# Index loads planned longer, first group's scatters behind the gathers, and the last 64 queries of two heads in quarters of TensorE

## The chip, the core and the metric

The kernel runs on one core of a Trainium2 chip. The metric is the device time of one execution in microseconds (us); the lower the better. Times of single instructions and waits are from the profile of one execution.

## The reference

The kernel computes three layers in one launch.

```python
# 1. attention, 4 batches x 8 heads, 576 queries and keys, 64 dims
scores = scale * q @ k.T
keep   = scores >= max(scores) - tau
attn   = softmax(where(keep, scores, -1e9));  x = attn @ v
# 2. dense layer on 2304 rows: 512 -> 2048 -> 512
h = x @ w_in;  x = (h * sigmoid(h)) @ w_out
# 3. one of 8 experts per row: 512 -> 1024 -> 512
e = argmax(normalised(x) @ normalised(expert_emb).T / tau2)
out[row] = gate(row) * (relu(x[row] @ w1[e]) @ w2[e])
```

## The kernel before

**Attention.** Heads go in pairs: 16 pairs (4 batches, 4 pairs each), 64 dims of one head on partitions 0 to 63 and of the other on 64 to 127. The 576 queries of a head are four chunks of 128 and a rest of 64. `score_pe` (L496) makes the scores of one chunk. For chunks 0 to 3 the two heads' products stand in the upper and lower 64 rows of TensorE and alternate, each head into its own bank of PSUM. The rest of both heads is one chunk, number 4: 64 queries of the first head and 64 of the second as the 128 columns of the stationary operand. In q, as the host lays it out, each of them has zeros in the other head's 64 rows, so one product over all 128 rows gives both. In the first eight pairs (`WIDE`, 72 steps) the 576 keys go in four pieces of 144, later in two of 288. Then DVE takes the maximum of each row (L519), ACT the exponential (L525), DVE masks and sums (L540), TensorE transposes (L577, L585, L593, L597) and multiplies with v (L669).

**Dense layer.** `moe_block` (L681) does six of sixteen hidden groups of 128 for a block of 256 rows beside the attention of later batches; `tail` (L1183) does the rest: three early blocks, then the other ten hidden groups of all nine blocks. Each hidden group is a product (L1117), tanh on ACT (L1337), a gate on DVE (L1342), a split into a high half on ACT (L1351) and a low half on POOL or DVE (L1354), and the second product (L1369).

**Experts.** The eight experts are sorted by the number of their rows. A table in DRAM collects the row numbers of each expert: POOL scatters 128 rows at a time into it (L1593). `turned` (L1842) then loads the indices of a group of rows (L1853, on SP), gathers the rows by them (L1860, indirect DMA from POOL), transposes them on TensorE (L1869) and splits them (L1875 on ACT, L1880 on DVE). `compute` (L1898) does the expert's two products (L1117 and L1928 or L1932), scales (L1967 on DVE, L1963 on ACT) and scatters the rows into the output (L1955, POOL). There are nine groups, 0 to 8. The weights of an expert are loaded in eight parts by SP (L1827) and split by ACT (L1094) and by DVE or POOL (L1098).

**What sets the order.** Every step is a task of a planner (`Plan`, L105) with an engine, a planned time, what it comes after, the buffers it takes and gives, and a rank. `Plan.run` (L220) walks through a planned time line: at each point it takes the task that can start first, among those that can start at about the same time the one of the lowest rank, and issues it then. So the planned times decide the order in which the instructions stand on each engine; on the chip each engine goes through its list in that order and waits where something is missing. `more` is a planned time from the end of a task to where its result is there (the way of a DMA). Tasks with `alt` go to the second engine if it is free earlier.

```python
t = plan.task("sp", 0.45, indices, [...], rank=..., more=1.8)      # L1882: index load
score = plan.task("pe", 1.18, partial(self.score_pe, ...), ...)    # L904
plan.task("pool", 1.03, partial(scatter, t, o), (x,), ...)         # L2001: into the output
```

Of the kernel before, what the change touches and what calls it, by code (L numbers as in the profile page):

```python
# [55 lines left out]
NBLK = NTOK // BLK  # L56
# [8 lines left out]
HALF = [slice(0, 64), slice(64, 128)]  # L65
# [195 lines left out]
class Kernel:  # L261
# [234 lines left out]
    def score_pe(self, st, ch, ws, uses):  # L496

        nc = self.nc
        for h, (w, use) in enumerate(zip(ws, uses)):
            w.nm = f"{ch}{h}" + st.nm  # L500
            bank = 3 if use.tag[0] == "B" else 0
            if use.wide:
                at = 512 * bank + 4 * APART * use.slot
                w.S = self.flat[:, at:at + 4 * APART].rearrange("p (a x) -> p a x", x=APART)[:, :, :PIECE]
            else:
                w.S = self.banks[:, bank:bank + 2, :288]
        lhsT = st.o.q[:, 128 * ch:128 * ch + 128]
        n, c = w.S.shape[1:]
        for a in range(n):
            for h, w in enumerate(ws):  # L510

                rows = HALF[h] if ch < 4 else slice(None)
                nc.tensor.matmul(  # L513
                    w.S[:, a], lhsT=lhsT[rows], rhs=st.o.k[rows, c * a:c * a + c], start=True, stop=True
                )

    def score_max(self, w):
# [367 lines left out]
    def attend(self, plan, pair, n, o, x_there):  # L885

        steps = self.steps(pair, o)
        st = steps[0][0]
# [4 lines left out]
        for a, step in enumerate(steps):  # L893
            s = 9.0 * n + a
            _, ch, h = step
            if h == 0:

                pe = []
                for i in range(2 if ch < 4 else 1):
                    w = Obj()  # L900
                    w.use = Token(f"{'AB'[i]}{(9 * n // 2 + n % 2 + (a + 1) // 2) % 2 if s < WIDE else 0}")
                    w.use.wide = s < WIDE
                    pe.append(w)
                score = plan.task(  # L904
                    "pe", 1.18, partial(self.score_pe, st, ch, pe, [w.use for w in pe]),
                    o.there + self.last_s + ([] if s < WIDE else self.last_wide),
                    tuple(w.use for w in pe), (o.k_use, o.q_use), rank=s - 0.6, slack=0.1, mode="scores",
                )
                self.last_s = [score]
                for x in (int(s) - 1, int(s)):  # L910
                    if x in self.held:
                        plan.link(score, self.held.pop(x))
            w = pe[h]
            scores, t = w.use, score
# [4 lines left out]
            t = plan.task("act", 0.84, partial(self.score_exp, w), (mx,), (use[2],), rank=s - 2, slack=0)  # L919
# [8 lines left out]
            for i, (tag, turn, pieces) in enumerate(self.turns(step)):  # L928
# [3 lines left out]
                give = [self.more_banks["T"]] if tag == "T" else []  # L932
# [871 lines left out]
    def experts(self, plan, const, last_job, u0, parts, halves, x2_taken, x_taken, seen, places, before):  # L1804
        nc = self.nc
# [36 lines left out]
        def turned(i, x_before):  # L1842

            rank, base, nt, p = SUBS[i]
            w = subs[i]
            n = nt * p
            r = units[i] - 4.0
            w.x_use = Token("X")
            w.x_there = []

            def indices():
                w.idx = self.pool.tile([128, nt, 2], I32, tag=f"idx{i}", bufs=1, name=f"idx{i}")
                nc.sync.dma_start(  # L1853
                    out=w.idx[:p],
                    in_=tbl[bass.ds(regs[rank], 1), base:base + nt * p].rearrange("o (p t) c -> (o p) t c", t=nt),
                )

            def gather(t, o):
                o.xg = self.pool.tile([128, ROW], F32, tag="s", bufs=BUFS["s"], name=f"xg{i}_{t}")[:, :DM]
                nc.gpsimd.indirect_dma_start(  # L1860
                    out=o.xg[:p], out_offset=None, in_=self.x2[:, :],
                    in_offset=bass.IndirectOffsetOnAxis(ap=w.idx[:p, t, 0:1], axis=0),
                )

            def turn(t, o, bank):
                if t == 0:
                    w.x = self.x_tiles(w.x_use, f"xe{i}", n)
                for kk in range(4):
                    nc.tensor.transpose(  # L1869
                        self.banks[:, bank.slot, p * kk:p * kk + p], o.xg[:p, 128 * kk:128 * kk + 128], self.ident[:p, :p]  # L1870
                    )

            def hi(t, bank):
                src = self.banks[:, bank.slot, :4 * p].rearrange("p (k x) -> p k x", k=4)
                nc.scalar.activation(out=w.x[0][:, :, p * t:p * t + p], in_=src, func=AF.Copy)  # L1875

            def lo(t, bank):
                to = (slice(None), slice(None), slice(p * t, p * t + p))
                src = self.banks[:, bank.slot, :4 * p].rearrange("p (k x) -> p k x", k=4)
                nc.vector.tensor_tensor(out=w.x[1][to], in0=src, in1=w.x[0][to].bitcast(F32), op=ALU.subtract)  # L1880

            t = plan.task("sp", 0.45, indices, [reg_there[rank]] + sum(places if i else places[:NBLK - 2], []), rank=r - (12 if i < 2 else 5), more=1.8)  # L1882
            us = p / 240 + 0.06, p / 240 + 0.08
            for j in range(nt):
                o, s_use, bank = Obj(), Token("s"), Token("M")
                x = plan.task("pool", 1.03, partial(gather, j, o), [t] + gathers[-1:], (s_use,), rank=r - (12 if i < 2 else 2) + 0.1 * j)
                gathers.append(x)
                x = plan.task("dma", 0.0, Obj, (x,), more=2.9)
                turns.append(plan.task(
                    "pe", 4 * p / 1200 + 0.01, partial(turn, j, o, bank), [x] + turns[-1:] + (x_before if j == 0 else []),  # L1890
                    (bank, w.x_use) if j == 0 else (bank,), (s_use,), rank=r,
                ))
                if j == 0:
                    x_taken.append(turns[-1])
                x = plan.task("act", us[0], partial(hi, j, bank), turns[-1:], (), (bank,), rank=r)
                w.x_there.append(plan.task("dve", us[1], partial(lo, j, bank), (x,), (), (bank,), rank=r))

        def compute(i):  # L1898
            rank, base, nt, p = SUBS[i]
            w = subs[i]  # L1900
# [89 lines left out]
            for t in range(nt):  # L1990
                o, row_use = Obj(), Token("rows")
                if by_rows:
                    bank, x = y_use[t], end[t]
                else:
                    bank = Token("M")
                    x = plan.task("pe", 0.43, partial(turn, t, bank), end, (bank,), (yT_use,), rank=r)
                x = plan.task(
                    "dve", 0.62, partial(scale, t, o, bank), [x] + before, (row_use,), (bank,), rank=r, alt=("act", 0.6)
                )
                before = [x]  # L2000
                plan.task("pool", 1.03, partial(scatter, t, o), (x,), give=(row_use,), rank=r, more=2.9)  # L2001

        before = weights(0, before)
        turned(0, x_taken[-1:])
# [78 lines left out]
```

## Time and profile before

| | us |
|---|---|
| median of three runs | 1062.93 |
| the three runs | 1062.93, 1062.95, 1058.68 |
| the profiled execution's own time | 1058.08 |
| its span from the first to the last instruction | 1056.3 |
| PE busy | 970.1 |
| DVE busy | 696.2 |
| ACT busy | 538.6 |
| POOL busy | 415.7 |

The span is one execution of the program on the chip. PE is TensorE's matmul, PEld its weight load, SP issues the DMAs of the loads and POOL the indirect ones. A wait is the idle time of an engine just before an instruction, with the instruction that ended it. A fp32 product shows as two MATMUL rows. TensorE's clock is granted at one of two levels, 1.2 and 2.4 GHz, which the profile gives as 0.50 and 1.00.

### The profile page before, as it was taken

The page shows a single profiled execution, that of the slowest core. Times are in us where ns is not written, and L with a number is a line of the kernel's source. Part 1 is how long each engine was busy: PE and PEld are TensorE (multiplying, and loading weights), DVE is VectorE, ACT ScalarE, POOL GpSimd, SP SyncE. Part 2 cuts the span into 40 slices and gives each one's busy share as a digit, 9 for nine tenths or more (in the row PEclk, how much of TensorE's full clock was granted, in tenths as well). Part 3 has the DMA queues.
Part 4 walks back from the last instruction along what each step waited for, and adds up shares of the span by engine and source line. Part 5 has one row for each costly group of instructions (what it writes and reads, how often), then busy time and mean ns, then how long its engine had stood idle before and what let it go on. Part 6 is the DMA issues. An engine that isn't in the chain of part 4 may idle for free. (4 is left out here: it accounts for less than half of the span.)

```text
span 1056.3 us, 18778 instructions
## 1 busy us (share of the span) xinstructions
PE 970.1 (92%) x6667; PEld 817.1 (77%) x6667; DVE 696.2 (66%) x1654; ACT 538.6 (51%) x1252; POOL 415.7 (39%) x406
## 2 busy tenths in 40 slices
PE   4878879999999899989999999999896999999995
PEld 4555566667667676878899889999786999899994
DVE  5779877878787886463388878777637445645521
ACT  4777776767676665363533333433534444344510
POOL 3565521445556640120154554443415434243210
PEclk9899999999999999999999999999998999999998
DMA  3234212454545421450532120212617745455400
GB/s 129 99 129 144 94 46 82 143 170 138 162 151 175 152 97 50 151 180 30 181 118 81 42 81 31 66 57 79 185 49 226 216 145 172 142 162 174 140 32 16
DMA packets 77633, 124.55 MB, mean 118 GB/s; under 512 B 11748, under 2 KB 38676, under 8 KB 77537
## 3 DMA queue, kind: packets, MB, share of 16 engines
q1 hardware_dynamic: 73089, 112.93, 33.8%
q0 software_dynamic: 4448, 10.40, 3.2%
q8 instruction: 53, 0.87, 0.3%
q14 instruction: 43, 0.35, 0.1%
HBM read 96.66 MB, written 27.45 MB: 117 GB/s over the span
## 5 line engine op out<-in xcount | busy, mean ns | idle before, releaser
L519 DVE TENSOR_REDUCE m<-banks 128x1 f32<-128x576 f32 x144 | 105.0, 752 | 34.0 <-PE banks L513 28.1
L540 DVE SCALAR_TENSOR_TENSOR P<-banks,m,e 128x576 f32<-128x576 f32 x128 | 103.5, 815 | 29.0 <-ACT e L525 16.2
L1094 ACT ACTIVATE whe<-rawe 128x512 fp32r<-128x512 f32 x128 | 76.6, 625 | 88.7 <-PE banks L1932 29.2
L1098 DVE TENSOR_TENSOR wle<-rawe,whe 128x512 fp32r<-128x512 f32 x93 | 68.4, 760 | 79.6 <-ACT whe L1094 72.7
L525 ACT ACTIVATE e<-banks,m 128x576 f32<-128x576 f32 x144 | 105.5, 733 | 14.0 <-PE banks L513 9.7
L513 PE MATMUL banks<-k,q 64*128 64x144 f32 (+3 forms) x792 | 98.2, 353 | 12.2 <-DVE m L519 4.9
L295 ACT ACTIVATE p<-banks 128x512 f32<-128x512 f32 (+2 forms) x164 | 75.3, 475 | 58.2 <-PE banks L577 39.3
L577 PE MATMUL banks<-ident,P 128*128 128x128 f32 x512 | 83.9, 288 | 22.3 <-ACT p L295 13.6
L1337 ACT ACTIVATE t<-banks 128x256 f32<-128x256 f32 x108 | 41.2, 382 | 122.7 <-PE banks L1117 119.5
L1117 PE MATMUL banks<-xs_6h,wh 128*128 128x256 f32 x360 | 102.4, 284 | 0.0
L1117 PE MATMUL banks<-xs_6h,wl 128*128 128x256 f32 x360 | 102.0, 283 | 0.0
L1117 PE MATMUL banks<-xs_6l,wh 128*128 128x256 f32 x360 | 101.9, 283 | 0.0
L577 PEld LDWEIGHTS banks<-ident,P 128*128 128x128 f32 x512 | 57.3, 144 | 52.4 <-ACT p L295 20.9
L669 PE MATMUL banks<-p,v 128*64 128x256 f32 (+3 forms) x640 | 91.6, 421 | 0.0
L513 PEld LDWEIGHTS banks<-k,q 64*128 64x128 f32 (+1 forms) x792 | 69.2, 195 | 28.1 <-DVE m L519 6.8
L1342 DVE SCALAR_TENSOR_TENSOR g<-t,banks 128x256 f32<-128x256 f32 x108 | 45.2, 419 | 58.8 <-ACT t L1337 47.4
L1098 POOL TENSOR_TENSOR wle<-rawe,whe 128x512 fp32r<-128x512 f32 x35 | 45.7, 1310 | 95.1 <-ACT whe L1094 79.2
L669 PEld LDWEIGHTS banks<-p,v 128*64 128x64 f32 (+1 forms) x640 | 41.4, 137 | 41.6 <-issue 19.5
L1117 PEld LDWEIGHTS banks<-xs_6h,wh 128*128 128x128 f32 x360 | 68.8, 191 | 3.1
L1117 PEld LDWEIGHTS banks<-xs_6l,wh 128*128 128x128 f32 x360 | 68.6, 190 | 3.0
L348 POOL TENSOR_TENSOR wa<-wa,wr 128x512 int32<-128x512 int32 x32 | 41.2, 1286 | 73.0 <-DVE wa L343 41.2
L1117 PEld LDWEIGHTS banks<-xs_6h,wl 128*128 128x128 f32 x360 | 68.5, 190 | 0.0
(560 smaller groups left out, 2833.1 us busy)
## 6 DMA issues: line engine op xcount, KB each, us to landing
rawe<-moe_w SPq DMA_DIRECT2D x64, 512.0 KB
wraw<-moe_w_in SPq DMA_DIRECT2D x16, 512.0 KB
wraw<-moe_w_out SPq DMA_DIRECT2D x16, 512.0 KB
wd<-wa SPq DMA_DIRECT2D x20, 256.0 KB
raw<-wd SPq DMA_DIRECT2D x10, 512.0 KB
q<-q SPq DMA_DIRECT2D x15, 320.0 KB
v<-v SPq DMA_DIRECT2D x16, 288.0 KB
x_dram<-t SPq DMA_DIRECT2D x16, 288.0 KB
```

Source lines behind the costliest of these rows:

```text
L295: self.nc.scalar.activation(out=out, in_=src, func=AF.Copy)
L348: nc.gpsimd.tensor_tensor(out=o.a, in0=o.a, in1=o.r, op=ALU.add)
L513: nc.tensor.matmul(w.S[:, a], lhsT=lhsT[rows], rhs=st.o.k[rows, c * a:c * a + c], start=True, stop=True)
L519: self.nc.vector.tensor_reduce(out=w.m[:, 0:1], in_=w.S, axis=AX.XY, op=ALU.max, negate=True)
L525: self.nc.scalar.activation(out=w.e, in_=w.S, func=AF.Exp, bias=w.m[:, 0:1])
L540: self.nc.vector.scalar_tensor_tensor(out=P.rearrange("p (a x) -> p a x", a=w.S.shape[1]), in0=w.S, scalar=w.m[:, 1:2], in1=w.e, op0=ALU.i ...
L577: nc.tensor.transpose(T[:, 128 * j:128 * j + 128], st.P[ch][:, c:c + 128], self.ident)
L669: nc.tensor.matmul(w.av[HALF[h], :nq], lhsT=st.o.vn[rows, k, :], rhs=st.pts[part][rows, k, :], start=(j == 0), stop=(j == 4),)
L1094: self.nc.scalar.activation(out=o.tiles[0][:, 2 * a:2 * a + 2], in_=o.raw[:, 2 * a:2 * a + 2], func=AF.Copy)
L1098: self.on[on].tensor_tensor(out=o.tiles[1][:, to], in0=o.raw[:, to], in1=o.tiles[0][:, to].bitcast(F32), op=ALU.subtract)
L1117: self.nc.tensor.matmul(h[:, :n], lhsT=lhs(a, kk), rhs=z[:, kk, :], start=(kk == 0 and i == 0), stop=(kk == 3 and i == 2))
L1342: nc.vector.scalar_tensor_tensor(out=o.g, in0=o.t, scalar=1.0, in1=self.banks[:, use.slot, :BLK], op0=ALU.add, op1=ALU.mult)
```

## The change

Chunk 4 becomes two products a piece: 64 rows by 64 columns in the upper left quarter of TensorE, and 64 by 64 in the lower right one, both into the same bank as before, on partitions 0 to 63 and 64 to 127. Its planned time goes from 1.18 to 0.65. The planned way of an index load goes from 1.8 to 3.5. The output scatters of group 0 come after the last gather that is planned before them, which is that of group 1. Six lines come in above L513, so that below it a line of the changed kernel has a number higher by six.

```diff
@@ score_pe
         lhsT = st.o.q[:, 128 * ch:128 * ch + 128]
         n, c = w.S.shape[1:]
+        if ch == 4:
+
+            for a in range(n):
+                for x in HALF:
+                    nc.tensor.matmul(
+                        w.S[x, a], lhsT=lhsT[x, x], rhs=st.o.k[x, c * a:c * a + c], start=True, stop=True
+                    )
+            return
         for a in range(n):
             for h, w in enumerate(ws):
-
-                rows = HALF[h] if ch < 4 else slice(None)
                 nc.tensor.matmul(
-                    w.S[:, a], lhsT=lhsT[rows], rhs=st.o.k[rows, c * a:c * a + c], start=True, stop=True
+                    w.S[:, a], lhsT=lhsT[HALF[h]], rhs=st.o.k[HALF[h], c * a:c * a + c], start=True, stop=True
                 )
@@ attend
                 score = plan.task(
-                    "pe", 1.18, partial(self.score_pe, st, ch, pe, [w.use for w in pe]),
+                    "pe", 1.18 if ch < 4 else 0.65, partial(self.score_pe, st, ch, pe, [w.use for w in pe]),
@@ turned
-            t = plan.task("sp", 0.45, indices, [reg_there[rank]] + sum(places if i else places[:NBLK - 2], []), rank=r - (12 if i < 2 else 5), more=1.8)
+            t = plan.task("sp", 0.45, indices, [reg_there[rank]] + sum(places if i else places[:NBLK - 2], []), rank=r - (12 if i < 2 else 5), more=3.5)
@@ compute
-                plan.task("pool", 1.03, partial(scatter, t, o), (x,), give=(row_use,), rank=r, more=2.9)
+                plan.task(
+                    "pool", 1.03, partial(scatter, t, o), [x] + (gathers[-1:] if i == 0 else []), give=(row_use,), rank=r, more=2.9
+                )
```

The planned times move instructions on all engines from the first pair to the second expert group; behind that (from expert group 3 on) the lists are the same. Three places are shown, each as the list of one engine before and now. Names end in a number of the buffer.

ACT, where the dense layer's early blocks begin after the last attention pair. `xs0_6h` is the high half of a block's input that a DMA brings, `wh` a high half of weights, `po5` the result of block 5, `t17_0` the tanh of the first hidden group of block 7, `ga7_0h` the high half that the second product waits for. Before:

```order
L1264 ACTIVATE xs0_6h_4658<-xc00_4660 128x2x256
L1094 ACTIVATE wh06_4691<-raw06_4664 128x512 x2
L1094 ACTIVATE wh16_4702<-raw16_4667 128x512
L1264 ACTIVATE xs0_6h_4658<-xc02_4680 128x2x256
L1094 ACTIVATE wh16_4702<-raw16_4667 128x512
L750 ACTIVATE po5_0_4723<-banks_99 128x512
L750 ACTIVATE po5_1_4729<-banks_99 128x512
L1337 ACTIVATE t17_0_4740<-banks_99 128x256
L1094 ACTIVATE wh08_4745<-raw08_4672 128x512 x2
L1337 ACTIVATE t17_1_4762<-banks_99 128x256
L1351 ACTIVATE ga7_0h_4768<-g17_0_4748 128x256
```

Now:

```order
L1270 ACTIVATE xs0_6h_4712<-xc00_4714 128x2x256
L1100 ACTIVATE wh06_4747<-raw06_4718 128x512
L756 ACTIVATE po5_0_4752<-banks_99 128x512
L756 ACTIVATE po5_1_4761<-banks_99 128x512
L1270 ACTIVATE xs0_6h_4712<-xc02_4736 128x2x256
L1343 ACTIVATE t17_0_4778<-banks_99 128x256
L1100 ACTIVATE wh06_4747<-raw06_4718 128x512
L1100 ACTIVATE wh16_4791<-raw16_4722 128x512
L1343 ACTIVATE t17_1_4798<-banks_99 128x256
L1357 ACTIVATE ga7_0h_4804<-g17_0_4786 128x256
```

The two results of block 5 and the weight halves no longer stand between the second input half (`xc02`) and the first tanh; between the tanh and `ga7_0h` there are still two weight halves and a tanh.

POOL, at the end of the last dense block (8), where the first expert group's rows are gathered. `gs8_8l` and `gs8_9l` are the low halves of hidden groups 8 and 9, `xg0_0` the first gather of group 0, which waits for the index load `idx0`. Before:

```order
L1593 DMA table_76<-ids_5705,at6_8163 19456x16 x2
L1354 TENSOR_TENSOR gs8_7l_8341<-g18_7_8307,gs8_7h_8340 128x256
L1354 TENSOR_TENSOR gs8_8l_8392<-g18_8_8379,gs8_8h_8391 128x256
L1860 DMA xg0_0_8413<-x2_75,idx0_8355 128x512
L1354 TENSOR_TENSOR gs8_9l_8421<-g18_9_8405,gs8_9h_8420 128x256
L1860 DMA xg0_1_8444<-x2_75,idx0_8355 128x512
```

Now:

```order
L1360 TENSOR_TENSOR gs8_7l_8291<-g18_7_8287,gs8_7h_8290 128x256
L1104 TENSOR_TENSOR wle0_0_8425<-rawe0_0_8314,whe0_0_8424 128x512 x2
L1360 TENSOR_TENSOR gs8_8l_8464<-g18_8_8447,gs8_8h_8463 128x256
L1866 DMA xg0_0_8507<-x2_75,idx0_8404 128x512
L1360 TENSOR_TENSOR gs8_9l_8502<-g18_9_8483,gs8_9h_8501 128x256
L1599 DMA table_76<-ids_5737,at7_8466 19456x16 x2
L1866 DMA xg0_1_8567<-x2_75,idx0_8404 128x512
```

The low half `gs8_9l` stands behind the gather as before, and two weight halves have come in ahead of it. On PE, of the 24 products of hidden groups 10 and 11 (`wh010`, `wl010`) three stood ahead of the products with group 8, three between those and the products with group 9, and 18 behind; now all 24 stand ahead of group 8's, and three of the next between the two. So PE has 21 more products to do before it needs `gs8_9l`. On SP one more register load stands ahead of the load of `idx0`.

POOL, at the end of expert group 0. `xg1_0` to `xg1_2` are the three gathers of group 1, `yr0_0` and `yr0_1` the scaled rows of group 0. Before:

```order
L1860 DMA xg1_0_8966<-x2_75,idx1_8931 96x512
L1860 DMA xg1_1_8980<-x2_75,idx1_8931 96x512
L1955 DMA out<-yr0_0_8978,idx0_8355 2304x512
L1860 DMA xg1_2_8987<-x2_75,idx1_8931 96x512
L1955 DMA out<-yr0_1_8982,idx0_8355 2304x512
L1098 TENSOR_TENSOR wle1_1_8704<-rawe1_1_8651,whe1_1_8703 128x512
L1098 TENSOR_TENSOR wle1_2_8719<-rawe1_2_8669,whe1_2_8718 128x512
```

Now:

```order
L1866 DMA xg1_0_9028<-x2_75,idx1_8979 96x512
L1866 DMA xg1_1_9030<-x2_75,idx1_8979 96x512
L1866 DMA xg1_2_9032<-x2_75,idx1_8979 96x512
L1104 TENSOR_TENSOR wle1_0_8727<-rawe1_0_8686,whe1_0_8726 128x512
L1961 DMA out<-yr0_0_9024,idx0_8404 2304x512
L1961 DMA out<-yr0_1_9026,idx0_8404 2304x512
```

The third gather no longer stands behind a scatter, and of two weight halves on POOL one is left. DVE, which had a weight half ahead of each of the three low halves of group 1's rows (`xe1l`, L1880) and two more ahead of them all, now has four ahead of the first and one between the first and the second.

## Rows read from the trace of the kernel before

**Rows 1.** Page, part 1: busy time, share of the span and instructions.
```profile
PE 970.1 (92%) x6667; PEld 817.1 (77%) x6667; DVE 696.2 (66%) x1654; ACT 538.6 (51%) x1252; POOL 415.7 (39%) x406
```

**Rows 2.** Busy time by stretch: length; engines with counts; granted clock, DMA share, GB/s.
```profile
20.00:190.00 170.00, 136.92 (x1165) 97.69 (x1165) 134.73 (x267) 121.00 (x279) 75.83 (x60) 0.95 0.30 97
...
746.10:749.50 3.40, 3.40 (x11) 2.94 (x12) 0.00 (x0) 0.00 (x0) 2.76 (x3) 0.50 0.90 303
...
797.30:807.60 10.30, 7.41 (x30) 6.82 (x31) 5.99 (x6) 3.52 (x7) 6.83 (x7) 0.50 0.93 279
...
452.60:456.00 3.40, 3.40 (x14) 3.01 (x13) 3.25 (x8) 3.27 (x9) 2.13 (x3) 0.50 0.95 297
```

**Rows 3.** Timeline, 447 to 452: start, length, engine, instruction, [idle before <-releaser].
```profile
447.28 0.63 ACT L1264 ACTIVATE xs_6h<-xc 128x512 fp32r<-128x512 f32 x1 [1.29 <-DMA xc<-x_dram]
447.82 0.61 ACT L1094 ACTIVATE wh<-raw 128x512 fp32r<-128x512 f32 x1
...
449.29 0.38 ACT L1337 ACTIVATE t<-banks 128x256 f32<-128x256 f32 x1
...
450.86 0.43 ACT L1351 ACTIVATE ga_0h<-g 128x256 fp32r<-128x256 f32 x1
...
451.35 0.49 PE L1369 MATMUL banks<-who,ga_0h 128*128 128x512 f32 x1 [3.02 <-ACT ga_0h L1351]
```

**Rows 4.** Timeline of PE, 311 to 314: a long wait inside the attention stage.
```profile
312.59 0.66 PE L577 MATMUL banks<-ident,P 128*128 128x128 f32 x4 [1.77 <-DVE P L540]
```

**Rows 5.** Timeline of POOL, 728 to 752: the first gather of group 0.
```profile
743.96 1.26 POOL L1860 DMA_INDIRECT xg<-x,idx  x1 [4.29 <-DMA idx<-table]
```

**Rows 6.** Timeline of PE, 726 to 752: 33 products in a row, then the wait.
```profile
734.85 0.36 PE L1117 MATMUL banks<-xs_6h,wh 128*128 128x256 f32 x1
...
738.88 0.39 PE L1369 MATMUL banks<-wh,gs_7h 128*128 128x512 f32 x1
...
746.03 0.74 PE L1369 MATMUL banks<-wh,gs_9l 128*128 128x512 f32 x1 [3.37 <-POOL gs_9l L1354]
```

**Rows 7.** Source L1799, SP's register loads: duration min/median/max in ns, first and last start.
```profile
L1799 SPq TENSOR_LOAD <-eint x8: 262/270/485, 733.8 to 740.8; - x8
```

**Rows 8.** Timeline of POOL, 780 to 815: gathers of group 1, scatters of group 0.
```profile
790.54 0.93 POOL L1860 DMA_INDIRECT xg<-x,idx  x1 [0.31 <-issue]
793.38 1.01 POOL L1955 DMA_INDIRECT out<-yr,idx  x1 [1.92 <-DVE yr L1967]
794.69 1.10 POOL L1860 DMA_INDIRECT xg<-x,idx  x1 [0.30 <-issue]
```

**Rows 9.** Timeline of PE, 792 to 802: the transposes of group 1.
```profile
793.75 0.55 PE L1869 MATMUL banks<-ident,xg 96*128 96x96 f32 x4 [0.42 <-DMA xg<-x,idx]
799.61 0.90 PE L1869 MATMUL banks<-ident,xg 96*128 96x96 f32 x4 [5.30 <-DMA xg<-x,idx]
801.09 0.61 PE L1117 MATMUL banks<-xe1h,whe 128*128 128x288 f32 x1 [0.58 <-ACT xe1h L1875]
```

**Rows 10.** Timeline of DVE, 792 to 802: scaled rows, weight halves, low halves.
```profile
792.35 1.44 DVE L1967 TENSOR_SCALAR yr<-banks,idx 128x512 f32<-128x512 f32 x2 [1.19 <-issue]
793.71 1.28 DVE L1098 TENSOR_TENSOR wle<-rawe,whe 128x512 fp32r<-128x512 f32 x2
...
796.44 3.74 DVE L1098 TENSOR_TENSOR wle<-rawe,whe 128x512 fp32r<-128x512 f32 x1
```

**Rows 11.** Timeline of PE, 185 to 187: chunk 4 before, and what follows it.
```profile
185.02 1.25 PE L513 MATMUL banks<-k,q 128*128 128x144 f32 x8
186.10 0.60 PE L577 MATMUL banks<-ident,P 128*128 128x128 f32 x4
```

**Rows 12.** Timeline of PE, 190 to 193: a chunk of two heads in 64 rows each.
```profile
191.08 1.24 PE L513 MATMUL banks<-k,q 64*128 64x288 f32 x8
192.25 0.49 PE L669 MATMUL banks<-p,v 128*64 128x320 f32 x2
```

**Rows 13.** PE by form, 30 to 440: count, busy us, mean ns of one, idle before.
```profile
L669 PE MATMUL banks<-p,v 64*64 64x320 f32 x64 | 12.1, 455 | 0.0
```

## Prediction

> **What bounds the kernel now.** I read the page's busy times first: TensorE is busy for 970.1 us of the span, 92%, DVE for 66% [rows 1]. So time is to be had only where TensorE idles or runs at half clock, and an edit that touches none of these can only cost. Next the busy times by stretch [rows 2]: from 20 to 190 us, the stage of the wide attention groups, TensorE is busy 136.92 of 170 us; there its 33 us of idle time belong to a chain over all engines (DVE alone 134.73), not to one wait. Later it hardly idles, except in three long waits. Each has its row with the engine that ended it: 3.02 us at 451.35 for ACT's high half of a gate [rows 3], 3.37 us at 746.03 for POOL's low half of a gate [rows 6], and 5.30 us plus 0.58 at 799.61 for a gather [rows 9]. And each is followed by a stretch at a granted clock of 0.50: 452.6 to 456.0, 746.1 to 749.5, 797.3 to 807.6, in which TensorE was busy 3.40, 3.40 and 7.41 us [rows 2]. At 1.00 the first two would have taken half as much, 1.7 us each. A wait of 1.77 us elsewhere had no stretch of half clock that I found behind it [rows 4]. So a wait costs its own length and perhaps as much again through the clock, and the change moves work in front of all three.
>
> **The change part by part.** The order lists show that it does move instructions, so "nothing changes" is not open.
>
> *The wait at 451.* Before, ACT took the second input half at 447.28, then weight halves and the two results of block 5, and only at 449.29 the tanh; the high half that TensorE waits for came at 450.86, 1.57 us after the tanh [rows 3]. Now the tanh stands right behind the input half, so it can start where a weight half started, 447.82. Between it and the high half stand as before two weight halves and a tanh, so 1.57 us again: 449.4 instead of 450.86. That takes 1.5 off the wait, which is then some 1.5 us, under the 1.77 that left the clock alone. Late instead are the weight halves for the next hidden groups, by one or two times 0.61, and TensorE has products of block 7 in front of those. The clock: none of the 1.7 us or all of it; I take half, -0.9, as DMA waits and weight halves keep the place thin. Together **-2.4** (bounds -1.5 and -3.2).
>
> *The wait at 746.* The chain is: index load, first gather (which waited 4.29 us for it [rows 5]), then the low half behind the gather on POOL, then TensorE. The longer planned way of the index load does not shorten that; it makes the planner put work in front of it. TensorE now has 21 more products to do before it needs the low half. 33 products in a row took 738.88 - 734.85 = 4.03 us, 0.122 each [rows 6]: 2.6 us. Against it one more register load stands ahead of the index load on SP. One takes 0.27 us, and eight of them started between 733.8 and 740.8, so 1.0 apart with what they wait for [rows 7]; I take 0.6. The wait falls by 2.6 - 0.6 = 1.9, to 1.45. Those 21 products were behind the wait before, so nothing is late for them; POOL's table scatter, which now stands between two gathers, and the two weight halves ahead of it lie under the same index wait. At 1.45, less than 1.77 [rows 4], I expect the clock to stay up: -1.7. Together **-3.6** (bounds -1.5, where the clock falls all the same, and -3.7).
>
> *The wait at 799.* Before, the second gather issued at 790.54, then a scatter that waited 1.92 for DVE and stood at 793.38, and only at 794.69 the third gather [rows 8]. Now the third follows the second: 790.54 + 0.93 + 0.30 = 791.8. From issue to the transpose that waited for it took 3.2 us for one gather (790.54 to 793.75) and 4.9 for another (794.69 to 799.61) [rows 8, 9]. So the rows would be there at 795.0 to 796.7, 2.9 to 4.6 earlier. But the change also puts four weight halves of 0.64 us (1.28 for two [rows 10]) on DVE ahead of the first low half of these rows, and one behind it. The scaled rows end at 793.7 [rows 10], so the first low half can start at 796.4, the third not before 798.3. One weight half here was stretched to 3.74 us [rows 10], beside POOL's work; with part of that the third comes at 799.6. The products, which started at 801.09 [rows 9], then start 1.5 to 2.8 earlier; I take -2.1. The two scatters of group 0 are some 2 us later, and nobody reads the output; their buffers are needed again in group 1, over 10 us on. In 797.3 to 807.6 TensorE was busy 7.41 us at half clock [rows 2], worth up to 3.7 less what was waited anyway; since a wait of some 3 us stays I take -1.0. Together **-3.1** (bounds -1.5, and -2.8 - 3.7 = -6.5).
>
> *The quarters.* A chunk 4 took 186.10 - 185.02 = 1.08 us to the start of the next operation: eight rows (four pieces, two rows each) some 0.13 apart [rows 11]. A chunk of two heads with 64 rows each, of as many columns in all, took 192.25 - 191.08 = 1.17 [rows 12]. The products with v already run in quarters: 64 rows, mean 455 ns, make 29.1 us if laid end to end, and 12.1 us busy [rows 13], so the two quarters run side by side, each at the length of its columns. Two quarters do in one pass what the one product with zeros did in one pass: no column is saved. I price a group at 1.17, +0.09, and with 16 groups **+1.4** (bounds 0 and, if quarters take turns, +1.08 each).
>
> The Trainium skill, page TensorEngine Tiling (Array Packing), section Theoretical Speedup, gives dimensions of at most 64 up to twice the speed. By that a group would take 0.54 and the sum would be 8.6 lower; that is rival B below. The trace so far does not bear it out for two quarters against one full product, since the product with zeros already holds both heads.
>
> *The planned 0.65.* The planner now thinks that chunk 4 ends 1.17 - 0.65 = 0.52 us sooner than it does. So what it issues behind it (the maximum on DVE, the next work on TensorE) is laid out too early, and an in-order engine waits behind it. Only the eight wide groups have idle time that this disturbs. The bounds are 0, where the idle time of 33 us takes it up, and 16 x 0.52 = 8.3. Next to them I have no row; the idle share of 19% [rows 2] lets me take 0.2 for each of eight groups, **+1.6**.
>
> **The sum:** -2.4 - 3.6 - 3.1 + 1.4 + 1.6 = -6.1. From the profiled execution's 1058.08 that is 1052.0. That execution lies with the fastest of the three runs; the median is 4.9 us above it, and from there the sum is 1056.8. As I can't say which of these levels the changed kernel will show, I predict the middle, **1054.4**, 0.8% under the median. A difference of 0.5%, 5.3 us, is about what a measurement can tell from none.
>
> **The rivals.**
>
> A. *The waits are only exchanged.* At 799 DVE's weight halves take the place of the gather, at 746 the index load comes a whole microsecond later, and the clock falls in all three places as before. For it: every stretch here has a DMA share of 0.90 to 0.95 [rows 2], and DVE's stretched half of 3.74 [rows 10]. Against it: 21 products are real work moved into the gap. The places then give -1.5 - 1.5 - 1.5, the quarters and plan take +3.0: -1.5, so 1056.6 to 1061.4. Chance 0.20, same.
>
> B. *Quarters run in half the time*, as the plan says (0.65). Then the +3.0 falls away, and 16 groups give 0.54 each, 8.6: 1058.1 - 9.1 - 8.6 = 1040, or 1045 if the wide stage, which waits for others, keeps its half. Against it: the two quarters of [rows 13] each take their full length. Chance 0.08, faster.
>
> C. *Quarters take turns*, because both write into one bank at once. Each group then doubles, +1.08, 16 times +17.3: 1058.1 - 9.1 + 1.6 + 17.3 = 1067.9. Slower. For it: the full chunks send each head into its own bank. Against it: both heads' products with v write one bank, and their rows overlap [rows 13]. It decides as soon as a group takes over 1.6 us. Chance 0.05. The Trainium skill, same page, section Restrictions and Gotchas, says that different row tiles write to different banks; by it this rival would hold, and the overlap in the trace speaks against it.
>
> D. *The wide stage loses*: slower. The planner's error of 0.52 us passes down the chain for all 16 groups, 8.3, the quarters cost 1.4, and the tail gives 1.5 at each of three places, -4.5, with no clock: +5.2, so 1063.3 from the profiled execution, 1068.1 from the median. The place is 20 to 190 us, and the point is where its 33 us of idle time grow by more than the tail gains. For it: everything there is issued in an order made from planned times, and DVE is 79% busy [rows 2]. Against it: an error of half a microsecond is small beside 33 us of slack. Chance 0.10.
>
> **How the numbers follow.** The forecast has 0.57: 0.40 of it faster, 0.17 within 0.5%, where a clock dip stays or the level is that of the median. With B faster is 0.48; with A same is 0.37; C and D make slower 0.15. The range: at the low end all three places at their best, -3.2 - 3.7 - 6.5 = -13.4, with costs between +1.4 and +3.0, give 1046.1 to 1047.7; 1047. At the high end 1064 takes in A from the median and D from the profiled execution. B, C and D from the median stay outside, under 0.2.
>
> **What would show it.** Right: a wait near 1.5 us at about 450 and at about 745, with a clock of 1.00 behind the second; the third gather of group 1 issued right behind the second; chunk 4 in 16 rows at about 1.17 us; idle time of TensorE from 20 to 190 within 2 us of 33. Wrong: a granted clock of 0.50 behind all three places (A), a chunk 4 at 0.6 (B) or above 1.6 (C), or over 5 us more idle time in the wide stage (D).

## The result and the profile after

The changed kernel takes 1068.05 us in the median of 20 runs (1062.67 to 1072.05), the kernel before 1060.88 in 20 runs of the same series. The ratio is 1.0068, with a 95% interval of 1.0051 to 1.0085: about 7 us **slower**, where 6 us faster was forecast. The time lies above the range. One of the 20 runs of the kernel before took 5201.01 us and has no part in the ratio.

The two profiled executions took 1058.08 and 1070.64 us, 12.6 apart, where the medians are 7.2 apart. So what follows, read from these two traces, shows where the time went, but makes the loss look some 5 us larger than it is.

The page's busy times of the changed kernel, in the columns of [rows 1]:

```profile
PE 986.4 (92%) x6763; PEld 820.8 (77%) x6763; DVE 700.8 (66%) x1639; ACT 540.0 (51%) x1260; POOL 422.6 (40%) x413
```

TensorE has 96 rows more (the quarters) and is busy 16.3 us longer. The span grew by 12.6, so over the whole kernel idle time is not what grew. The busy times by stretch say where. The attention stage is taken from the start of the span to the last product with v, which stood at 428.5 us and now stands at 444.6; the columns are those of [rows 2]. Before:

```profile
0.00:186.00 186.00, 142.83 (x1201) 102.89 (x1202) 140.38 (x279) 125.92 (x286) 79.91 (x68) 0.95 0.32 103
0.00:428.50 428.50, 375.51 (x2830) 270.80 (x2832) 332.44 (x667) 287.54 (x670) 195.16 (x165) 0.98 0.38 122
```

After, in the same two stretches (the first ends with the last scores of a wide group) and in the one from 20 to 190:

```profile
0.00:200.40 200.40, 153.35 (x1239) 109.03 (x1241) 140.51 (x282) 127.09 (x290) 75.53 (x64) 0.86 0.28 91
0.00:444.60 444.60, 392.68 (x2928) 275.50 (x2928) 329.23 (x656) 289.58 (x678) 196.48 (x168) 0.93 0.36 118
...
20.00:190.00 170.00, 135.25 (x1107) 94.26 (x1108) 126.18 (x253) 113.21 (x263) 70.22 (x55) 0.88 0.27 87
```

The attention stage is 16.1 us longer. Its idle time of TensorE is 428.5 - 375.5 = 53.0 before and 444.6 - 392.7 = 51.9 now. Its busy time is 17.2 us more for the same products (at most 1.6 of it is the quarters' own time, worked out below), at a mean granted clock of 0.93 instead of 0.98. So over the stage the loss is paid in clock. Most of it, 200.4 - 186.0 = 14.4 us, lies ahead of 200 us, where the clock went from 0.95 to 0.86. Up to there idle time grew too, from 186.0 - 142.8 = 43.2 to 200.4 - 153.4 = 47.0 us; behind that TensorE waits some 5 us less than before, so the sum over the stage stays.

Behind the attention stage the kernel took 1056.3 - 428.5 = 627.8 before and takes 1068.9 - 444.6 = 624.3 now, 3.5 us less. That is less than half of the 9.1 that the three waits were to bring, and no more than single executions differ: the run of the quarters alone (below), which has the old order there, took 1056.2 - 432.9 = 623.3. The three places in the changed kernel, TensorE's timeline:

```profile
465.90 0.50 PE L1375 MATMUL banks<-who,ga_0h 128*128 128x512 f32 x1 [1.52 <-ACT ga_0h L1357]
...
763.38 0.50 PE L1375 MATMUL banks<-wh,gs_9l 128*128 128x512 f32 x1 [0.57 <-POOL gs_9l L1360]
...
807.00 1.19 PE L1875 MATMUL banks<-ident,xg 96*128 96x96 f32 x8 [0.73 <-DMA xg<-x,idx]
...
808.77 0.40 PE L1123 MATMUL banks<-xe1h,whe 128*128 128x288 f32 x1 [0.58 <-ACT xe1h L1881]
...
811.98 0.61 PE L1123 MATMUL banks<-xe1l,whe 128*128 128x288 f32 x1 [2.81 <-DVE xe1l L1886]
...
821.13 0.61 PE L1938 MATMUL banks<-he_0h,whe 128*128 128x288 f32 x1 [4.11 <-ACT he_0h L1921]
...
822.58 0.61 PE L1938 MATMUL banks<-he_0l,whe 128*128 128x288 f32 x1 [0.84 <-DVE he_0l L1924]
```

and the stretches behind them (length, TensorE busy, ..., granted clock):

```profile
467.70:471.10 3.40, 3.40 (x15) 3.10 (x14) 3.15 (x8) 2.32 (x7) 1.27 (x1) 0.50 0.62 210
755.00:775.00 20.00, 18.63 (x129) 16.68 (x128) 14.26 (x31) 12.95 (x31) 13.49 (x12) 1.00 0.73 233
809.00:815.80 6.80, 3.99 (x17) 3.82 (x17) 4.22 (x8) 1.54 (x3) 4.66 (x5) 0.50 0.95 306
819.30:826.10 6.80, 4.13 (x15) 3.81 (x16) 4.59 (x7) 4.44 (x9) 1.27 (x1) 0.50 0.79 224
```

The wait near 451 is 1.52 instead of 3.02 [rows 3], but a half-clock stretch still follows. The one of 3.37 near 746 [rows 6] is down to 0.57, and there the clock stays at 1.00. The 5.30 for the third gather [rows 9] became 0.73 and 2.81; then a wait of 4.11 came up that was 0.24 in the kernel before, in the lines behind those of [rows 9]:

```profile
808.26 0.40 PE L1932 MATMUL banks<-he_0h,whe 128*128 128x288 f32 x1 [0.24 <-ACT he_0h L1915]
809.71 0.40 PE L1932 MATMUL banks<-he_0l,whe 128*128 128x288 f32 x1 [1.05 <-DVE he_0l L1918]
```

ACT's timeline names what ended the 4.11:

```profile
819.63 1.15 ACT L1100 ACTIVATE whe<-rawe 128x512 fp32r<-128x512 f32 x2 [3.06 <-DMA rawe<-moe_w]
820.68 0.39 ACT L1921 ACTIVATE he_0h<-banks 128x288 fp32r<-128x288 f32 x1
```

The high half `he_0h` stands on ACT behind two weight halves, and those waited 3.06 us for a load. The waits shown from the transposes to `he_0l` make 0.73 + 0.58 + 2.81 + 4.11 + 0.84 = 9.1 us, where before they were 5.30 + 0.58 + 0.24 + 1.05 = 7.2; the third place brought nothing.

### The profile page after: what moved, and what is told of

The parts are those of the page before. It is cut to its first block, busy times and chain, and to the rows that moved or that the text cites. A ratio compares the mean times of both kernels' runs of the same rounds, so it can differ in the third digit from the quotient of the medians.

```text
span 1068.9 us, 18974 instructions
## 1 busy us (share of the span) xinstructions
PE 986.4 (92%) x6763; PEld 820.8 (77%) x6763; DVE 700.8 (66%) x1639; ACT 540.0 (51%) x1260; POOL 422.6 (40%) x413
## 5 line engine op out<-in xcount | busy, mean ns | idle before, releaser
L1104 DVE TENSOR_TENSOR wle<-rawe,whe 128x512 fp32r<-128x512 f32 x93 | 64.2, 716 | 80.1 <-ACT whe L1100 71.0
L295 ACT ACTIVATE p<-banks 128x512 f32<-128x512 f32 (+2 forms) x172 | 80.8, 488 | 69.1 <-PE banks L583 52.3
L583 PE MATMUL banks<-ident,P 128*128 128x128 f32 x512 | 86.7, 294 | 22.7 <-DVE P L546 11.3
L675 PE MATMUL banks<-p,v 128*64 128x256 f32 (+3 forms) x640 | 99.2, 450 | 0.0
L519 PE MATMUL banks<-k,q 64*128 64x144 f32 (+1 forms) x704 | 81.5, 360 | 5.7 <-DVE m L525 3.1
L675 PEld LDWEIGHTS banks<-p,v 128*64 128x64 f32 (+1 forms) x640 | 44.2, 148 | 47.8 <-issue 26.7
L519 PEld LDWEIGHTS banks<-k,q 64*128 64x128 f32 x704 | 56.7, 199 | 20.7 <-issue 7.9
```

The lines of the kernel that those rows point to most:

```text
L295: self.nc.scalar.activation(out=out, in_=src, func=AF.Copy)
L519: nc.tensor.matmul(w.S[:, a], lhsT=lhsT[HALF[h]], rhs=st.o.k[HALF[h], c * a:c * a + c], start=True, stop=True)
L583: nc.tensor.transpose(T[:, 128 * j:128 * j + 128], st.P[ch][:, c:c + 128], self.ident)
L675: nc.tensor.matmul(w.av[HALF[h], :nq], lhsT=st.o.vn[rows, k, :], rhs=st.pts[part][rows, k, :], start=(j == 0), stop=(j == 4),)
L1104: self.on[on].tensor_tensor(out=o.tiles[1][:, to], in0=o.raw[:, to], in1=o.tiles[0][:, to].bitcast(F32), op=ALU.subtract)
```

## The experiments

Two theories at first. **P**: the planned 0.65 gives the wide stage another order, and that order costs the clock. **Q**: the quarters do, because they keep less of TensorE at work, or cost time themselves. Each run was timed in rounds beside the kernel before on the same chip; a ratio is against that.

### Only the planned time, only the quarters, only the tail, and all but the planned time

```diff
# e1_plan_only: the old product
-                    "pe", 1.18, partial(self.score_pe, ...
+                    "pe", 1.18 if ch < 4 else 0.65, partial(self.score_pe, ...
# e2_quarters_only: the quarters in score_pe, "pe", 1.18
# e3_tail_only: old product at 1.18; more=3.5; scatters of group 0 behind gathers[-1:]
# e4_true_plan: the changed kernel with
-                    "pe", 1.18 if ch < 4 else 0.65, partial(self.score_pe, ...
+                    "pe", 1.18, partial(self.score_pe, ...
```

Expected of the first: 

> Chunk 4 keeps the one product with zeros over 128 rows; only its planned time is 0.65 instead of 1.18. Theory P (the planned time reorders the wide stage, and the order brings the stretches of half clock): 12 to 16 us slower than the kernel before, ratio 1.011 to 1.015, with 45 us or more of granted clock 0.50 before 200 us (17 us in the kernel before). Theory Q (quarter products, which keep a smaller part of TensorE at work, bring the half clock): no slower than 1.002, about 17 us of half clock before 200 us.

Of the second: 

> Chunk 4 in quarters, planned at 1.18 as before: the order of every engine is that of the kernel before, only the products differ. Theory P: +1.5 us from the quarters' own time (1.13 against 1.08 in eight groups, 1.12 against 0.97 in eight), ratio 1.000 to 1.003, half clock before 200 us as in the kernel before. Theory Q: 12 us or more slower, ratio above 1.010.

Of the third: 

> Old product, planned at 1.18; only the index load's planned way of 3.5 and the scatters of group 0 behind the gather. If the tail's gain stands by itself (theory P and Q alike): 3 to 5 us faster, ratio 0.995 to 0.997, with the wait near 746 below 1.8 us and the one near 800 below 4. If the gain at the gather needed the other order of the attention stage too: ratio 0.999 to 1.001.

Of the fourth: 

> The changed kernel with chunk 4 planned at 1.18, so with quarters, the index latency and the scatter order, but the old order of the attention stage. Theory P: the sum of the two runs before, 1.5 to 3.5 us faster than the kernel before, ratio 0.996 to 0.999, so some 9 us faster than the changed kernel. Theory Q: as slow as the changed kernel, ratio 1.006 to 1.012.

| | median us | ratio | 95% interval |
|---|---|---|---|
| planned 0.65 alone | 1068.97 | 1.0081 | 1.0055 to 1.0108 |
| quarters alone | 1058.49 | 0.9994 | 0.9966 to 1.0022 |
| index load and scatters alone | 1054.35 | 0.9937 | 0.9916 to 0.9958 |
| all but the planned 0.65 | 1053.83 | 0.9943 | 0.9920 to 0.9966 |
| the change | 1068.05 | 1.0068 | 1.0051 to 1.0085 |

P holds and Q falls. A number in the planner, with every product as it was, makes the kernel slower by as much as the whole change; the quarters cost nothing that these runs can tell; and the change without that number is faster than the kernel before by 0.57%. The loss came out smaller than the 1.1% that P expected, the tail's gain larger than expected. The stretches of the attention stage, of 0.65 alone, the quarters alone and the tail alone, each to its last product with v:

```profile
0.00:442.30 442.30, 388.70 (x2830) 278.71 (x2832) 329.75 (x656) 290.55 (x678) 196.84 (x168) 0.93 0.37 118
```
```profile
0.00:432.90 432.90, 381.92 (x2927) 268.34 (x2928) 330.08 (x667) 287.00 (x670) 195.38 (x165) 0.97 0.37 121
```
```profile
0.00:430.30 430.30, 378.19 (x2830) 271.64 (x2832) 329.50 (x667) 287.49 (x670) 196.10 (x165) 0.96 0.37 121
```

Idle time of TensorE is 53.6, 51.0 and 52.1 us, within 3 us of both kernels; over the stage, busy time and clock are what differ. With 0.65 alone the stage has exactly the 2830 rows of the kernel before and is busy 13.2 us longer. The stretches of granted clock 0.50 in it, added up, in the kernel before and with 0.65 alone:

```profile
sum 17.00, PE 15.71 PEld 11.52 DVE 10.75 ACT 10.72 POOL 8.23; mean PE 3.93 PEld 2.88 DVE 2.69 ACT 2.68 POOL 2.06
```
```profile
sum 61.20, PE 51.44 PEld 35.21 DVE 41.55 ACT 37.64 POOL 21.55; mean PE 6.43 PEld 4.40 DVE 5.19 ACT 4.71 POOL 2.69
```

TensorE was busy for 35.7 us more at half clock; half of that, 17.9 us, is what the clock can cost, and it is enough for the 13.2.

The index load and the scatters bring 1060.44 - 1054.35 = 6.1 us in the medians (4.5 to 8.9 by the interval). The tail alone has, behind its attention stage, 1048.2 - 430.3 = 617.9 us, 9.9 less than the kernel before, but only 5.4 less than the quarters alone with 623.3; all but the planned 0.65 has 1050.0 - 433.3 = 616.7. With the planned 0.65 besides, 6 to 8 us of that are lost again in the profiles, since the order it makes runs into the tail: the wait of 4.11 near 821 is in neither of these two. In the tail alone the wait at the first place is as long as before, the one at the second has moved to the gathered rows, and what stays near 800 is mostly one wait for DVE:

```profile
453.37 0.50 PE L1369 MATMUL banks<-who,ga_0h 128*128 128x512 f32 x1 [3.26 <-ACT ga_0h L1351]
...
751.52 1.12 PE L1869 MATMUL banks<-ident,xg 128*128 128x128 f32 x4 [2.51 <-DMA xg<-x,idx]
...
799.12 0.61 PE L1117 MATMUL banks<-xe1l,whe 128*128 128x288 f32 x1 [3.61 <-DVE xe1l L1880]
```

### The index load alone, the scatters alone

```diff
# e7_index_only: more=1.8 -> more=3.5, else the kernel before
# e8_scatter_only: [x] + (gathers[-1:] if i == 0 else []), else the kernel before
```

> Only the index load's planned way, 3.5 instead of 1.8. By the recorded terms (1.9 us of the wait near 746 and up to 1.7 of its clock): 2 to 3.6 us faster, ratio 0.9966 to 0.998; the wait near 800 stays above 5 us. If the gain of the two edits together is the scatters': 0.9985 to 1.0005.

> Only the scatters of group 0 behind the last gather of group 1. By the recorded terms (2.1 us of the wait near 800 and 1.0 of its clock): 2 to 4 us faster, ratio 0.996 to 0.998; the wait near 746 stays at 2.7 to 3.4 us. If DVE's weight halves take the gather's place: 0.9985 to 1.0005, with the wait near 800 of the same length but ended by DVE.

The index load alone: 1058.67 us, ratio 0.9983 (0.9961 to 1.0005). The scatters alone: 1057.59, 0.9973 (0.9944 to 1.0003). Neither is clear of no change by itself, both together are. TensorE's timeline tells more than the times. The index load alone:

```profile
756.06 1.11 PE L1869 MATMUL banks<-ident,xg 128*128 128x128 f32 x4 [3.66 <-DMA xg<-x,idx]
```

and the scatters alone:

```profile
801.00 0.55 PE L1869 MATMUL banks<-ident,xg 96*128 96x96 f32 x4 [0.65 <-DMA xg<-x,idx]
803.73 0.61 PE L1117 MATMUL banks<-xe1h,whe 128*128 128x288 f32 x1 [2.18 <-ACT xe1h L1875]
...
805.55 0.61 PE L1117 MATMUL banks<-xe1l,whe 128*128 128x288 f32 x1 [1.20 <-DVE xe1l L1880]
```

With the index load alone the wait for the low half is only exchanged for one of 3.66 on the gathered rows themselves, a little further on. With the scatters alone the 5.30 is gone; in its place stand shorter waits that follow each other, 0.65 for gathered rows, 2.18 for ACT and 1.20 for DVE, so a part of it was exchanged there too. Each edit leaves the other's wait as long as it was or longer: 6.04 us for the third gather with the index load alone, 3.79 us for the low half with the scatters alone.

### Where in the attention stage, and is it the error's size?

```diff
# e5_plan_wide
+                    "pe", 0.65 if ch == 4 and s < WIDE else 1.18, ...
# e12_plan_narrow
+                    "pe", 0.65 if ch == 4 and s >= WIDE else 1.18, ...
# e6_plan_late
+                    "pe", 1.71 if ch == 4 else 1.18, ...
# e11_plan_1_00
+                    "pe", 1.0 if ch == 4 else 1.18, ...
```

> Old product; the planned 0.65 for chunk 4 in the eight wide groups only, 1.18 in the eight narrow ones. If the loss sits in the wide stage: ratio 1.007 to 1.015 as with 0.65 in all 16, with 45 us or more of half clock before 200 us. If it needs the narrow groups' order too: under 1.003.

> Old product; the planned 0.65 in the eight narrow groups only, 1.18 in the wide ones. TensorE idles little there, so its order costs or gains little: ratio 0.997 to 1.003, half clock before 200 us as in the kernel before. If the narrow groups' order carries a part of the gain that the run with 0.65 in the wide groups alone missed: 3 to 6 us faster.

> Old product; chunk 4 planned at 1.71, so wrong by as much as 0.65 but on the other side (what follows is laid out too late). If too early is what hurts (an in-order engine stands at an instruction whose bank is not free yet): ratio 0.998 to 1.003, half clock before 200 us of at most 30 us. If any other order of the wide stage loses, because the order before was a lucky one: ratio above 1.006.

> Old product; chunk 4 planned at 1.00, within 0.08 of the 1.08 it takes in the wide groups. It moves about as many instructions of the wide stage as 0.65 does. If the size of the error decides: ratio 0.998 to 1.002. If any other order of the wide stage loses against the one before: ratio 1.004 to 1.012.

| chunk 4 planned at | median us | ratio | 95% interval |
|---|---|---|---|
| 0.65, wide groups only | 1078.76 | 1.0182 | 1.0151 to 1.0214 |
| 0.65, narrow groups only | 1064.42 | 1.0022 | 0.9997 to 1.0048 |
| 1.71 in all | 1071.64 | 1.0093 | 1.0057 to 1.0129 |
| 1.00 in all | 1067.61 | 1.0055 | 1.0030 to 1.0080 |

The theory that "too early" hurts fell: too late by the same half microsecond costs as much, and a planned time within 0.08 of the true one still costs 0.55%. Three of the planned times make an order of the wide stage that differs from the one before (0.65 makes the same one in all groups and in the wide ones alone); all of them are slower. The fourth, 0.65 in the narrow groups, leaves the wide stage's order as it was and can't be told from no change. So it is not the size or the sign of the planner's error: the order of the kernel before is better than the three others tried. Whether any other order would lose is not shown.

Where the loss sits is shown for 0.65 only. The last scores of a wide group start at 199.6 us with it in all groups and at 197.2 in the wide ones alone; with the old order of the wide stage they start at 185.0 to 193.1 in the seven runs that have it. With 1.71 and 1.00 they start at 193.9 and 193.4, too near to that to tell. 0.65 in the wide groups alone is worse than in all 16, so the parts do not add: from those last scores to the last product with v it takes 449.1 - 197.2 = 251.9 us, with 0.65 in all groups 442.3 - 199.6 = 242.7. Idle time over its attention stage has grown too, to 449.1 - 391.6 = 57.5 us from the 53.0 of the kernel before:

```profile
0.00:449.10 449.10, 391.55 (x2832) 278.46 (x2832) 336.08 (x664) 288.30 (x674) 190.61 (x164) 0.93 0.36 116
```

What the orders do to TensorE is seen in one pair. The timeline of the kernel before, its waits between 50 and 66 us:

```profile
51.68 1.25 PE L513 MATMUL banks<-k,q 128*128 128x144 f32 x8 [0.82 <-DVE m L519]
...
54.63 0.66 PE L577 MATMUL banks<-ident,P 128*128 128x128 f32 x4 [1.26 <-ACT p L295]
...
63.95 0.55 PE L593 MATMUL banks<-ident,Pm 64*128 64x64 f32 x5 [1.52 <-ACT p L295]
...
65.39 0.66 PE L577 MATMUL banks<-ident,P 128*128 128x128 f32 x4 [0.65 <-ACT p L295]
```

The changed kernel in the same pair:

```profile
54.94 1.20 PE L513 MATMUL banks<-k,q 64*64 64x144 f32 x16 [1.82 <-DVE P L546]
...
68.62 1.08 PE L583 MATMUL banks<-ident,P 128*128 128x128 f32 x4 [3.81 <-DVE P L546]
```

Chunk 4 now waits until DVE has masked the scores whose place it takes; then what stands behind it is done nearly in one go, and TensorE waits 3.81 us at once for DVE. Many short waits became few long ones, and in this pair their sum is larger: with one of 0.17 before and one of 0.40 now that are not shown, 4.4 us became 6.0. The four transposes behind the 3.81 took 1.08 us instead of 0.66, for the clock was at half:

```profile
68.62:69.70 1.08, 1.08 (x6) 0.75 (x8) 1.08 (x3) 1.05 (x4) 0.48 (x1) 0.50 0.20 42
```

### Filling the waits

```diff
# e9_plan_filled on the planned 0.65 alone, e10_tail_filled on the tail alone
+        for _ in range(self.FILL[kind].get(k, 0)):
+            self.nc.tensor.transpose(self.flat[:, 1400:1528], self.ident, self.ident)
```

> The kernel of the run with the planned 0.65 alone, order untouched, and in it 126 more transposes of the identity on TensorE, into free columns of PSUM that nothing reads: 5 to 24 of them right ahead of each of eleven instructions that waited 0.9 to 3.8 us between 28 and 202 us, sized to about three quarters of that wait. If the long waits bring the half clock: half clock between 30 and 200 us falls from 47 us to under 25, and the kernel gains 4 to 10 us on its own base, ratio to the kernel before 0.999 to 1.005. If the half clock does not depend on these waits: as slow as its base or slower, ratio 1.008 or more.

> The index and scatter edits with the old product and the old order, and 88 such transposes ahead of ten waits of 1.1 to 2.8 us in the wide stage. If waits bring the half clock: half clock between 30 and 200 us (17 us without them) under 8, 2 to 4 us faster than the two edits alone, ratio 0.989 to 0.992. If not: 0.993 to 0.998.

This can't decide the question. The filling transposes waited themselves, for DVE's work on the bank in which they write, and then stood in the way. TensorE by form, 28 to 205 us, and the timeline at 67:

```profile
L503 PE MATMUL banks<-ident 128*128 128x128 f32 x126 | 21.1, 332 | 16.9 <-DVE P L550 14.5 <-ACT e L535 1.7 <-DVE Pm L550 0.7
```
```profile
67.77 4.38 PE L503 MATMUL banks<-ident 128*128 128x128 f32 x24 [3.72 <-DVE P L550]
```

The wait of 3.81 before the pair's transposes is now 3.72 before the filling, whose 24 transposes then take 4.38 us. The kernel is slower than its base, 1081.44 us, ratio 1.0196 (1.0157 to 1.0234), though its clock from 30 to 200 us is a little higher, 0.91:

```profile
30.00:200.00 170.00, 138.01 (x1133) 104.86 (x1129) 119.31 (x241) 107.47 (x250) 64.18 (x51) 0.91 0.27 87
```

Without the filling that order has 0.86 (0.65 alone), 0.88 (in the wide groups only) and 0.89 (the change) in the same stretch, so in single executions the rise is too small to be called shown. The tail with filling, 1053.09 us, 0.9912 (0.9877 to 0.9947), can't be told from the tail without, and both have a clock of 0.95 there. That the long waits bring the half clock is therefore argued from the rows and not shown; why these orders lower the clock stays open. It was not tried with filling that waits for nothing, as there is no bank of PSUM there that no other engine reads.

## Why the prediction was wrong

**The step that failed** is the planned 0.65, priced at +1.6 (0.2 us of a 0.52 us error for each of eight groups). It measured +8.5 us by itself (1068.97 against 1060.44), as much as the bound of 8.3, and some 14 us on top of the other edits (1068.05 against 1053.83, in two series whose kernels before had 1060.88 and 1060.44), far beyond it. The prediction sized it by what the instruction is late, and bounded it by that error times the groups. Both were the wrong measure: the planned time counts by the order that it makes. That the order is the cause is shown; the traces show the cost as busy time at half clock, with some 4 us of idle time in the wide stage that the narrow groups give back.

**Rival D** had the sign, the place and nearly the number (1063.3 to 1068.1), with a chance of 0.10. Its mechanism was half right: the wide stage loses and outweighs the tail, but mostly through the clock and not because "its 33 us of idle time grow". From 20 to 190 us the idle time is 170 - 135.25 = 34.8, within the 2 us that I had named as a sign of being right. That window was badly chosen, as the stage now ends 14 us later; up to its end idle time grew by some 4 us, from 43.2 to 47.0, under the 5 that D asked for. The clock of 0.88 in the same row was the sign to name. That 8.3, an error of 0.52 us times 16 groups, comes near the 8.5 is luck: the same error in eight groups alone cost 1078.76 - 1059.48 = 19.3 us.

**The quarters** were priced rightly in the sum: a group takes 1.08 to its successor at the end of the wide stage, 199.57 to 200.65, and 1.13 in most wide groups (1.08 before), 1.12 in the narrow ones (0.97 before); over 16 groups 8 x 0.05 + 8 x 0.15 = 1.6 at the most, +1.4 forecast. The runs bound it less well: the quarters alone measured 2 us less than the kernel before, with an interval from 3.6 less to 2.3 more. Rivals B and C are out:

```profile
199.57 1.15 PE L513 MATMUL banks<-k,q 64*64 64x144 f32 x16
200.65 1.03 PE L675 MATMUL banks<-p,v 128*64 128x320 f32 x6
```

Sixteen rows in 1.08 us are two at a time into one bank: in the trace two rows start within 0.01 us, the next two 0.12 us later, which is also the distance of two full rows before. (The overlap of [rows 13] did not show this by itself: the eight full rows of [rows 11] last 0.30 us each on average, 2.4 us end to end, and take 1.25.) The Trainium skill, page TensorEngine Tiling (Array Packing), section Theoretical Speedup, would have allowed up to twice the speed; no run here shows it. The Trainium skill, same page, section Restrictions and Gotchas, says that different row tiles do not use one bank at once; here two quarters in different rows, on different partitions of the bank, do, without a loss.

**The three waits** of the changed kernel were read rightly at two places: 1.52 at the first as forecast, the second gone with its clock; at the third the gather stands right behind the second one. Too hopeful were the half of the first one's clock (a stretch of 3.40 us is still there, behind a wait shorter than the 1.77 of [rows 4], so that wait was no bound) and, above all, the third place: -3.1 became nothing, since a weight load that comes late took over at 821. That is in the changed kernel only. That the tail alone has 9.9 us less in its profile, where -9.1 was forecast, is luck: its first wait is as long as before, 3.26, its second is 2.51, now for the gathered rows, where 1.45 was forecast, and against the quarters alone it has 5.4 us less.

**Rival A** held in part: the clock fell behind the first and the third place as before, and at the third DVE's low half came late (2.81), as A said; the 4.11 for ACT's weight halves behind a DMA A did not have.

## What to carry to other kernels

In a kernel whose order comes from a planner, a planned time is a handle on the order and no measurement: before such a number is touched, compare the orders it gives, and time it alone, even when the edit that it belongs to costs nothing. Where TensorE idles in many short waits, price a new order by the granted clock of the stage as well as by idle time; over the attention stage idle time was the same to 1 us here, and 16 us were lost in the profiled pair. The version to keep is the change without the 0.65: 1053.83 us with quarters, 1054.35 without, which these runs can't tell apart, both faster than either kernel.

## What was not expected of the hardware

The seven kernels with the old order in the wide stage, in single executions, had mean clocks of 0.92 (0.65 in the narrow groups) to 0.96 (the kernel before) from 30 to 200 us, and ended their attention at 428.5, 430.3 (tail alone), 434.9 (index load alone) and 434.3 us (scatters alone). One profiled execution thus stands for a spread of 6 us, and the kernel before's was at its lower end. The clock of the first microseconds is no mark of the order either: from 13.7 to 27.3 it was 0.87 in the kernel before and 0.50 in the changed one, but 0.50 also with the tail, the index load or the scatters alone. In the stretch from 30 to 200 the kernels with the order of 0.65 lie below all of the seven, at 0.86 to 0.89, and 1.71 and 1.00 at 0.89 and 0.91. The row of 0.65 alone:

```profile
30.00:200.00 170.00, 136.57 (x1074) 96.71 (x1071) 123.97 (x250) 111.29 (x260) 64.57 (x51) 0.86 0.27 86
```

A long wait alone does not decide it: in the kernel before 2.77 us of waiting at 113.09 left the clock at 1.00.

```profile
113.09 0.65 PE L577 MATMUL banks<-ident,P 128*128 128x128 f32 x4 [2.77 <-ACT p L295]
```
```profile
113.09:116.50 3.41, 3.41 (x24) 1.67 (x24) 2.75 (x8) 2.77 (x7) 2.12 (x2) 1.00 0.12 45
```
